# An attention-and-FFN kernel whose hash test moves into the contraction of its scores, in another layout, with its reciprocals through DRAM and in a free order

## The chip, the cores and the metric

The kernel runs on one core of a Trainium2 chip. The metric is the device time of one execution in microseconds (us), lower is better. The kernel before and the changed kernel were timed alternately; "before" and "changed" below always mean these two. Times are medians of all runs, slow ones too; a ratio is the mean time of one kernel's fast runs over that of the other's fast runs of the same rounds on the same chip, so it is not quite the ratio of the medians that stand beside it. Engines: PE is TensorE, DVE is VectorE, ACT is ScalarE, POOL is GpSimd, SP is the engine that only issues DMAs.

## The reference

Attention over 4 batches, 8 heads, 768 positions and 64 dimensions, in which a query sees only the keys of the same hash bucket (six sign bits), followed by a maxout FFN.

```python
q_bits = (np.einsum('bhsd,dk->bhsk', q, proj) > 0)      # proj: 64 x 6
k_bits = (np.einsum('bhsd,dk->bhsk', k, proj) > 0)
mask   = q_bucket[:, :, :, None] == k_bucket[:, :, None, :]
scores = np.where(mask, scale * q @ k.T, -1e9)
attn   = exp(scores - max) / sum                          # then attn @ v
h      = np.maximum(np.maximum(x @ w1, x @ w2), x @ w3)   # x: 3072 x 512, w: 512 x 768
out    = h @ w_out
```

## The kernel before

Its work comes in 16 phases (batch, four heads, half of the queries). In each phase PE makes the scores of the present phase in six groups, and between the groups it does the denominators and AV of the phase before and pieces of the FFN of the batch before. The order on every engine is the order of the source (`manual_schedule`). The 64 dimensions of a head lie as two blocks of 32 rows, so that four heads fill the 128 rows and a third round adds the hash test: a mismatch in any of 12 rows (six bits and their complements) adds -512.

```python
    def qk_group(ph, b, pp, half, c):
        scs = [scp.tile([P, 2, 512], FP32, tag="sc", name="sc") for _ in (0, 1)]
        qs = slice(half * HS, half * HS + HS)
        ks = slice(c * P, c * P + P)
        kT = tr["k", b, pp][:].bitcast(BF16).rearrange("p a (n two) -> p a n two", two=2)[:, :, :, 1]
        qT = tr["q", b, pp][:].bitcast(BF16).rearrange("p a (n two) -> p a n two", two=2)[:, :, :, 1]
        for rnd in range(3):
            for g in range(4):
                rows = slice(32 * g, 32 * g + 32)
                if rnd < 2:
                    l, r = kT[rows, rnd, ks], qT[rows, rnd, qs]
                else:
                    l, r = bits["k", b, pp][rows, ks], bits["q", b, pp][rows, qs]
                nc.tensor.matmul(scs[g // 2][:, g % 2, 0:HS], l, r, start=(rnd == 0), stop=(rnd == 2))
        for jj in (0, 1):
            nc.scalar.activation(atile(ph, jj, c)[:, :, 0:HS], scs[jj][:, :, 0:HS], ActFn.Exp, scale=SCALE)
```

The denominators are summed by PE with a matrix of ones, so each of four row groups of 32 holds one head. Their reciprocal and its broadcast over 64 rows stay on chip: 32x32 transposes on VectorE, and eight small copies on GpSimd.

```python
    def den(ph, b, pp, half):
        ps = bank()
        for c in range(NCH):
            for jj in (0, 1):
                for hd in (0, 1):
                    g = 2 * jj + hd
                    nc.tensor.matmul(ps[32 * g : 32 * g + 32, 0:HS], ones32[:],
                                     atile(ph, jj, c)[:, hd, 0:HS],
                                     start=(c == 0), stop=(c == NCH - 1))
        ds = dp.tile([P, HS], FP32, tag="ds", name="ds")
        nc.vector.tensor_scalar(out=ds[:], in0=ps[:, 0:HS], scalar1=float(S) * EPS, scalar2=None, op0=AluOp.add)
        dT = dp.tile([P, HS // 32, 32], FP32, tag="dT", name="dT")
        nc.vector.transpose(dT[:].rearrange("p a x -> p (a x)"), ds[:])
        rc = dp.tile([P, HS // 32], FP32, tag="rc", name="rc")
        nc.vector.reciprocal(rc[:], dT[:, :, 0])
        for jj in (0, 1):
            r2 = dp.tile([P, HS // 32], FP32, tag=f"r2{jj}", name=f"r2{jj}")
            for hd in (0, 1):
                for e in (0, 1):
                    o = 64 * hd + 32 * e
                    s = 32 * (2 * jj + hd)
                    nc.gpsimd.tensor_copy(r2[o : o + 32, :], rc[s : s + 32, :])
            rb = dp.tile([P, HS], FP32, tag=f"rb{jj}", name=f"rb{jj}")
            nc.vector.transpose(rb[:].rearrange("p (a x) -> p a x", x=32),
                                r2[:, :, None].to_broadcast([P, HS // 32, 32]))
            rcb[ph, jj] = rb
```

AV then multiplies by this `rb` while it leaves PSUM (`xT = (AV + eps * sum(v)) * rb`):

```python
# ... (matmuls into ps left out)
        nc.vector.scalar_tensor_tensor(
            out=xT[b][:, 2 * pp + jj, half * HS : half * HS + HS], in0=ps[:, 0:HS],
            scalar=sv[:, 0:1], in1=rcb.pop((ph, jj))[:], op0=AluOp.add, op1=AluOp.mult)
```

The hidden tile of the FFN gets its first value by a cast (`h`, line 281, on VectorE except in the tail) and two maxima on VectorE (line 284). The whole kernel:

The softmax here doesn't subtract the row's maximum and nothing guards it: scores larger than these inputs give would overflow.

## Time and profile before

366.1 us median (365.8 to 371.4, four runs; the longest is a slow run, over 1.5% above the fastest); one profiled run spans 363.1 us. The first fence is from the page of the kernel before: the span, busy time by engine, and four rows of the 40 time slices (tenths busy; the last is the granted clock of PE in tenths).

```profile
span 363.1 us, 7556 instructions
...
PE 300.6 (83%) x3166; PEld 131.1 (36%) x3166; DVE 203.4 (56%) x364; ACT 162.3 (45%) x223; POOL 39.1 (11%) x176
...
PE   5688688669797886989898795979998897999685
...
DVE  1625987665536668557245877567345554273531
ACT  1169289135556352510666653520496654701121
...
PEclk9689999899989996999989999899999998999999
```

PE is busy 83% of the span and is the engine to look at. But a busy PE is not a full one: matmuls overlap, so the groups below have 334 ns as the mean of one matmul though they start 162 ns apart. The costliest groups (line, engine, operation, output<-inputs, shapes, count | busy us, mean ns | idle before):

```profile
L272 PE MATMUL wk<-xT,w_sb 128*128 128x384 f16 x540 | 107.2, 334 | 30.2 <-DVE h_1882 L281 3.8
...
L202 PE MATMUL sc<-qT,kT 32*128 32x384 bf16 x768 | 59.8, 344 | 10.9 <-DVE bx L178 2.3
...
L202 PE MATMUL sc<-qb,kb 32*128 32x384 bf16 x384 | 37.4, 332 | 0.1
...
L167 PE MATMUL bps<-qT,pmq 32*32 32x384 f32 x256 | 21.6, 552 | 5.8 <-DVE sv L259 4.3
...
L150 DVE STREAM_TRANSPOSE kT<-knat 128x768 f32<-128x768 f32 (+1 forms) x18 | 25.1, 1437 | 0.0
```

The timeline around 200 us shows what a score group costs (start, duration, engine, line, operation, count):

```profile
start us, us, engine line op out<-in xcount [idle before <-releaser]
...
199.70 0.34 PE L202 MATMUL sc<-qT,kT 32*128 32x384 bf16 x4
199.87 0.33 PE L202 MATMUL sc<-qb,kb 32*128 32x384 bf16 x4
...
200.13 0.82 PE L272 MATMUL wk<-xT,w_sb 128*128 128x384 f16 x4
...
200.88 0.73 PE L202 MATMUL sc<-qT,kT 32*128 32x384 bf16 x8
```

Four heads' matmuls start at once, in four groups of 32 rows, and the next four 0.17 us later. The step to the FFN (line 272), which uses the whole array, takes 0.26 us (199.87 to 200.13) instead of some 0.16.

Since busy time misleads, I also split the time between PE's first and last matmul in three, from the trace: **wait** is the time in which no matmul was in flight (gaps over 50 ns); **clock** is half of the rest that lies in stretches of halved clock; **own** is what is left: the matmuls at their pace, with the changes of array mode. For the kernel before: own 285.6, clock 14.8, wait 57.3 us.

### The profile page before, as it was taken

How to read it: one execution, taken by the hardware profiler on the slowest of the kernel's cores; microseconds unless marked ns; L12 is line 12 of the kernel's file. 1: busy time of each engine (PE TensorE's matmuls, PEld its weight loads, DVE VectorE, ACT ScalarE, POOL GpSimd, SP SyncE). 2: the span in 40 equal slices, each digit the busy share in tenths (PEclk: the TensorE clock that was granted, in tenths of full speed). 3: DMA queues.
4: the chain of work that ended last, by engine and by line, in shares of the span. 5: the costliest groups of instructions: out<-in, count | busy, mean ns of one | idle time of the engine just before them, and what ended most of it. 6: DMA issues, size and time to landing. Idle time of an engine off the chain costs nothing. (4 is left out here: it accounts for less than half of the span.)

```text
span 363.1 us, 7556 instructions
## 1 busy us (share of the span) xinstructions
PE 300.6 (83%) x3166; PEld 131.1 (36%) x3166; DVE 203.4 (56%) x364; ACT 162.3 (45%) x223; POOL 39.1 (11%) x176
## 2 busy tenths in 40 slices
PE   5688688669797886989898795979998897999685
PEld 1123133224343432445343342335443342454342
DVE  1625987665536668557245877567345554273531
ACT  1169289135556352510666653520496654701121
POOL 7003013010301011000103103000011101000100
PEclk9689999899989996999989999899999998999999
DMA  8999243132025103130563003111200000102002
GB/s 181 296 302 199 36 185 44 29 123 93 10 52 198 49 2 43 40 106 10 183 253 45 2 0 45 60 51 46 88 2 0 2 3 0 70 19 88 2 0 87
DMA packets 17858, 27.62 MB, mean 76 GB/s; under 512 B 1952, under 2 KB 12960, under 8 KB 17824
## 3 DMA queue, kind: packets, MB, share of 16 engines
q1 hardware_dynamic: 10784, 20.85, 16.1%
q0 software_dynamic: 6720, 6.29, 11.0%
q8 instruction: 24, 0.39, 0.5%
q14 instruction: 10, 0.08, 0.1%
q10 hardware_dynamic: 320, 0.01, 0.0%
HBM read 25.17 MB, written 6.29 MB: 87 GB/s over the span
## 5 line engine op out<-in xcount | busy, mean ns | idle before, releaser
L272 PE MATMUL wk<-xT,w_sb 128*128 128x384 f16 x540 | 107.2, 334 | 30.2 <-DVE h_1882 L281 3.8
L272 PEld LDWEIGHTS <-w_sb 128*128 128x128 f16 x576 | 53.1, 98 | 89.8 <-issue 58.4
L202 PE MATMUL sc<-qT,kT 32*128 32x384 bf16 x768 | 59.8, 344 | 10.9 <-DVE bx L178 2.3
L292 ACT COPY o<-wk 128x512 f32<-128x512 f32 x23 | 13.5, 586 | 64.4 <-PE wk L289 44.1
L202 PE MATMUL sc<-qb,kb 32*128 32x384 bf16 x384 | 37.4, 332 | 0.1
L202 PEld LDWEIGHTS <-kT 32*128 32x128 bf16 x768 | 15.1, 94 | 53.2 <-issue 48.6
L255 PEld LDWEIGHTS <-v 128*64 128x64 f16 x384 | 20.3, 112 | 17.8 <-issue 11.4
L167 PE MATMUL bps<-qT,pmq 32*32 32x384 f32 x256 | 21.6, 552 | 5.8 <-DVE sv L259 4.3
L167 PE MATMUL bps<-kT,pmk 32*32 32x384 f32 x256 | 20.8, 553 | 5.9 <-DVE kT L150 4.0
L150 DVE STREAM_TRANSPOSE kT<-knat 128x768 f32<-128x768 f32 (+1 forms) x18 | 25.1, 1437 | 0.0
L150 DVE STREAM_TRANSPOSE qT<-qnat 128x768 f32<-128x768 f32 (+1 forms) x18 | 24.7, 1387 | 0.0
L259 DVE TENSOR_SCALAR sv<-wk 128x1 f32<-128x1 f32 x31 | 4.9, 157 | 33.6 <-PE wk L255 33.6
L231 DVE TENSOR_SCALAR ds<-wk 128x384 f32<-128x384 f32 x15 | 8.3, 556 | 25.6 <-PE wk L227 25.6
L202 PEld LDWEIGHTS <-kb 32*128 32x128 bf16 x384 | 12.9, 94 | 7.5 <-issue 1.5
L204 ACT ACTIVATE at_127<-sc 128x768 f16<-128x768 f32 x8 | 6.5, 815 | 18.7 <-PE sc L202 18.6
L204 ACT ACTIVATE at_159<-sc 128x768 f16<-128x768 f32 x8 | 6.5, 814 | 18.7 <-PE sc L202 18.7
L204 ACT ACTIVATE at_171<-sc 128x768 f16<-128x768 f32 x8 | 6.5, 814 | 16.0 <-PE sc L202 15.9
L178 DVE TENSOR_SCALAR kb<-bps,thrk 128x384 bf16<-128x384 f32 x10 | 6.2, 617 | 12.8 <-PE bps L167 12.8
L227 PEld LDWEIGHTS <-ones_121 128*32 128x32 f16 x384 | 8.9, 96 | 9.0 <-issue 5.5
L167 PEld LDWEIGHTS bps<-kT,pmk 32*32 32x32 f32 x256 | 6.7, 110 | 14.3 <-DVE kT L150 5.0
L85 POOL DMA_DIRECT2D v<-in_v_dram x16 | 11.6, 726 | 0.8 <-POOLq L400 0.8
L204 ACT ACTIVATE at_143<-sc 128x768 f16<-128x768 f32 x8 | 6.5, 814 | 11.4 <-PE sc L202 11.4
(440 smaller groups left out, 529.0 us busy)
## 6 DMA issues: line engine op xcount, KB each, us to landing
out_dram<-o SPq DMA_DIRECT2D x24, 256.0 KB, 2.0
knat<-in_k_dram SPq DMA_DIRECT2D x7, 768.0 KB, 5.2
qnat<-in_q_dram SPq DMA_DIRECT2D x7, 768.0 KB, 7.5
v<-in_v_dram POOLq DMA_DIRECT2D x16, 192.0 KB, 4.0
w_sb<-in_moe_w_dram POOLq DMA_DIRECT2D x3, 768.0 KB, 23.2
qb<-bx SPq DMA_DIRECT2D x14, 72.0 KB, 2.0
knat<-in_k_dram SPq DMA_DIRECT2D x2, 384.0 KB, 6.5
qnat<-in_q_dram SPq DMA_DIRECT2D x2, 384.0 KB, 9.0
```

The source lines that it names most:

```text
L85: nc.gpsimd.dma_start(t[:].rearrange("p h c d -> p h (c d)"), v[b, 2 * j : 2 * j + 2].rearrange("h (p c) d -> p h (c d)", p=P))
L150: nc.vector.transpose(t[:, blk, c0 * P : c1 * P].rearrange("p (c i jj) -> p jj c i", jj=4, i=32), n[:].rearrange("p (jj c x) -> p jj c x", ...
L167: nc.tensor.matmul(ps[o : o + 32, :], pm[nm][32 * g : 32 * g + 32, blk, :], tr[nm, b, pp][32 * g : 32 * g + 32, blk, cs], start=(blk == 0) ...
L178: nc.vector.tensor_scalar(out=d, in0=ps, scalar1=thr[nm][:, 0:1], scalar2=(1.0 if nm == "q" else MISS), op0=AluOp.is_gt, op1=AluOp.mult)
L202: nc.tensor.matmul(scs[g // 2][:, g % 2, 0:HS], l, r, start=(rnd == 0), stop=(rnd == 2))
L204: nc.scalar.activation(atile(ph, jj, c)[:, :, 0:HS], scs[jj][:, :, 0:HS], ActFn.Exp, scale=SCALE)
L227: nc.tensor.matmul(ps[32 * g : 32 * g + 32, 0:HS], ones32[:], atile(ph, jj, c)[:, hd, 0:HS], start=(c == 0), stop=(c == NCH - 1))
L231: nc.vector.tensor_scalar(out=ds[:], in0=ps[:, 0:HS], scalar1=float(S) * EPS, scalar2=None, op0=AluOp.add)
L255: nc.tensor.matmul(ps[D * hd : D * hd + D, 0 : HS + 1], vv[:, hd, c, :], atile(ph, jj, c)[:, hd, :], start=(c == 0), stop=(c == NCH - 1))
L259: nc.vector.tensor_scalar(out=sv[:], in0=ps[:, HS : HS + 1], scalar1=EPS, scalar2=None, op0=AluOp.mult)
L272: nc.tensor.matmul(ps[:, 0:HS], w_sb[m][:, jc, fb * P : fb * P + P], xT[b][:, jc, half * HS : half * HS + HS], start=(jc == 0), stop=(jc = ...
L292: nc.scalar.copy(o[:], ps[:, 0:DM])
```

## The change

Each head gets a full pass of the array: its 64 dimensions and its 12 hash rows lie side by side in one operand of 76 rows (first head of a pair) or 128 rows (second head: hash rows, zeros, dimensions). With it come other changes: batch 0 is transposed by PE instead of VectorE, phases are pairs of heads (both query halves), PSUM is one pool of four two-bank tiles, the first cast of `h` is always on ScalarE, q and k are loaded by GpSimd with overlapping rows, the reciprocal goes through three DMA steps and DRAM (the last step is four broadcasts), and `manual_schedule` is gone, so that the framework orders the instructions of each engine by its own estimate ("free order"). The core of the diff:

```diff
-    scp = ctx.enter_context(tc.tile_pool(name="scp", bufs=3, space=bass.MemoryType.PSUM))
-    wkp = ctx.enter_context(tc.tile_pool(name="wkp", bufs=2, space=bass.MemoryType.PSUM))
-    ctx.enter_context(tc.manual_schedule())
+    drp = ctx.enter_context(tc.tile_pool(name="drp", bufs=3, space=bass.MemoryType.DRAM))
+    psp = ctx.enter_context(tc.tile_pool(name="psp", bufs=4, space=bass.MemoryType.PSUM))
 ...
+    HROW = (D, 0)
+    KROWS = (slice(0, D + 2 * NBITS), slice(0, P))
 ...
+    def hash_bits(b, js):
+        pst = [psum2("bps") for _ in js]
+        for half in (0, 1):
+            cs = slice(half * HS, half * HS + HS)
+            for x, (j, ps) in enumerate(zip(js, pst)):
+                for hd in (0, 1):
+                    rows = slice(D * hd, D * hd + D)
+                    for z, nm in enumerate(("q", "k")):
+                        o = 32 * (2 * (hd ^ x) + z)
+                        nc.tensor.matmul(ps[o : o + 32, half, 0:HS], pm[nm][rows, :],
+                                         oset(b, j)[nm, hd][rows, cs], start=True, stop=True)
+        # ... one VectorE op makes the bits (bt), four DMAs put them into the operands' hash rows
 ...
+    def qk_unit(ph, b, j, half, c):
+        sc = psum2("sc")
+        for hd in (0, 1):
+            rows = KROWS[hd]
+            kT = oset(b, j)["k", hd].bitcast(BF16)[:, 1::2]
+            qT = oset(b, j)["q", hd].bitcast(BF16)[:, 1::2]
+            nc.tensor.matmul(sc[:, hd, 0:HS], kT[rows, c * P : c * P + P],
+                             qT[rows, half * HS : half * HS + HS], start=True, stop=True)
+        nc.scalar.activation(atile(ph, half, c)[:, :, 0:HS], sc[:, :, 0:HS], ActFn.Exp, scale=SCALE)
 ...
     def den(ph):   # after the matmuls with ones
+        nc.scalar.copy(ds[:], ps[:, 0:HS])
+        E = HS // 32
+        cd = dp.tile([P, E], FP32, tag="cd", name="cd")
+        nc.sync.dma_start(cd[:], ds[0:P:32, :].rearrange("g (m e) -> g m e", e=E))
+        rc = dp.tile([P, E], FP32, tag="rc", name="rc")
+        nc.vector.tensor_scalar(out=rc[:], in0=cd[:], scalar1=float(S) * EPS, scalar2=None, op0=AluOp.add)
+        nc.vector.reciprocal(rc[:], rc[:])
+        rd = drp.tile([4, HS], FP32, tag="rd", name="rd")
+        nc.sync.dma_start(rd[:].rearrange("g (m e) -> (g m) e", e=E), rc[:])
+        for half in (0, 1):
+            rb = dp.tile([P, HS], FP32, tag=f"rb{half}", name=f"rb{half}")
+            for hd in (0, 1):
+                g = 2 * half + hd
+                nc.sync.dma_start(rb[D * hd : D * hd + D, :], rd[g : g + 1, :].to_broadcast([D, HS]))
+            rcb[ph, half] = rb
 ... (loads, transposes, output DMAs and the order of emission are left out)
```

## The prediction

> **What bounds the kernel now.** The engine table gives PE 300.6 us of a 363.1 us span, DVE 203, ACT 162. But PE is not working all that time. From the timeline, undisturbed start-to-start paces are 162 ns for a full-array 384-column matmul, 165 ns for a group of four row- or column-tiled ones, and 216 ns for a 512-column one. The change of array mode adds about 95 ns (252 to 260 ns instead of 162); the Trainium skill, "TensorEngine Tiling (Array Packing)", section "Key Properties", says that changing the tiling mode drains the engine, and the trace agrees. At those paces all PE work is about 245 us. The rest is waiting: 57 us of PE gaps over 0.1 us, about 18 us for 200 mode changes, some 10 us of halved clock (mean 0.952), a 17 us start before the first exponential, and PE waiting on DVE evictions behind 1.6 us transposes (1 to 4 us gaps before the first FFN layer).
> By exponentials in the timeline: start 17 us, batch 0 57 us, twelve later phases 20.1 us each, tail 47 us.
>
> **What the change does on PE.** Scores: 288 groups of four (47.5 us at pace) become 384 full-array passes, 62 us: 15 us MORE ideal work, although the record of busy time (97 us) suggests a saving. Hash: 512 records become 256, in 64-row tiles of four at a time: about 25 us instead of 32. Transposes of batch 0: 48, estimated 5 to 10 us. FFN, denominators and AV keep 93+31+15+31 us. Total about 265 us. Scores now share the mode of the FFN; mode changes in the built order fall only from 201 to 170.
>
> **Elsewhere.** DVE: transposes 48 x 1.57 = 75 us (was 50, two heads per instruction now), but denominator transposes, broadcast transposes and the h casts leave: about 190 us in all. ACT: 192 x 0.81 + 48 x 0.48 casts + 24 x 0.59 + 16 x 0.48 = about 200 us. The reciprocal path now crosses three DMAs (each about 2 us to landing in the DMA issues), about 11 us from the denominators to xT; the order leaves room for most of it. q/k are read twice for batches 1 to 3.
>
> **Critical path, estimated.** Start 21 us (256-byte loads, transposes, hash and the DMA of hash rows before the first score). Phases 0 to 4 have no FFN and are bound by ACT: 12 x 0.81 + 0.5 = 10.2, so about 11 us each, plus 3 to 5 us because the loads of pairs 1 and 2 come late and PE is in order: ends near 80 us (before: 93). Eleven phases with FFN: qk 4.0 + den 1.0 + AV 2.0 + hash 1.5 + FFN 7.7 + mode changes 0.8 = 17 us of PE; with 8% for waits and clock, 18.4: 202 us. Tail: 40 us FFN plus latency, 46 us.
> Sum 328 us. So the gain comes from the free order, the shared PSUM pool (four two-bank tiles instead of three plus two single banks) and a fuller batch 0, not from the score pass.
>
> **Prediction 328 us, 80% range 308 to 349. Faster by over 2%: 0.88; within 2%: 0.08; slower: 0.04.**
>
> **What would show it.** Score matmuls at 162 ns pace; PE total at pace higher, gaps halved; exponentials back to back in the first five phases; no 1 to 4 us gaps before the first FFN layer; phases of 18 to 19 us; tail unchanged.
>
> **What would make it wrong.** xT waiting for the broadcast DMA and blocking the in-order DVE queue, so that maxima, PSUM tiles and PE wait (phases of 20 us or more); late 256-byte loads stalling the start past 30 us; strided score operands slower at full array; or, to the good, hardly any waits (310 us).

## The result, and the profile after

The changed kernel takes 435.6 us median (429.7 to 438.0, four runs, of which that of 438.0 counts as slow) against 366.1: ratio 1.185, 95% interval 1.170 to 1.200. It is 18% slower; 328 us had been predicted. From its page, the rows that answer to those of before:

```profile
span 434.2 us, 5976 instructions
...
PE 354.0 (82%) x2186; PEld 158.9 (37%) x2186; DVE 160.8 (37%) x290; ACT 188.7 (43%) x281; POOL 105.7 (24%) x223
...
PE   6489496929399789679797997979698799799994
...
DVE  5073331331235462344325334434414432233341
ACT  1064356605236365245364272626255167432231
...
PEclk9596857976679999699889698969789699999999
```

VectorE and ScalarE are far from full (37% and 43%), PE is as busy as before by its share, and the clock row has 5s, 6s and 7s in 13 of its 40 slices where the kernel before had two 6s and otherwise 8s and 9s: the mean granted clock is 0.865, where it was 0.952. The groups:

```profile
L294 PE MATMUL wk<-xT,w_sb 128*128 128x384 f16 x576 | 120.4, 344 | 12.1 <-DVE xT L284 7.9
...
L220 DVE TENSOR_SCALAR bt<-bps,thr,fac 128x768 f32<-128x768 f32 x16 | 17.2, 1077 | 60.3 <-PE bps L216 60.3
...
L239 PE MATMUL sc<-qop_0_126,kop_0_123 76*128 76x384 bf16 x72 | 26.3, 366 | 9.4 <-DMA kop_0_123<-bt 6.5
...
L239 PE MATMUL sc<-qop_0_127,kop_0_124 128*128 128x384 bf16 x72 | 26.3, 368 | 0.0
...
L216 PE MATMUL bps<-qop_0_126,pmq 64*32 64x384 f32 x24 | 12.6, 619 | 9.1 <-DVE qop_0_126 L202 6.9
```

The split of PE's time: own 309.2 (before 285.6), clock 44.7 (14.8), wait 74.3 (57.3). So of 71 us, 24 are more work on PE, 30 are a slower clock and 17 more waiting. By line, the 24 are the hash matmuls (22 to 35 us), the scores (68 to 74), the new transposes on PE (6) and small changes elsewhere, with the FFN's first layer 5 us cheaper.

What does PE wait for? One phase, from the timeline of all engines ("SPq" is the issue of a DMA; in brackets the idle time before an instruction and what ended it):

```profile
start us, us, engine line op out<-in xcount [idle before <-releaser]
...
297.16 0.33 PE L251 MATMUL wk<-at_187,ones_117 128*32 128x384 f16 x2
...
297.59 0.48 ACT L255 COPY ds<-wk 128x384 f32<-128x384 f32 x1 [2.44 <-PE wk L251]
...
300.08 0.59 SPq L258 DMA_DIRECT2D cd<-ds  x1
...
302.87 0.55 DVE L303 TENSOR_TENSOR h_2638<-h_2638,wk 128x384 f16<-128x384 f16 x1 [1.38 <-PE wk L294]
...
303.34 0.17 DVE L260 TENSOR_SCALAR rc<-cd 128x12 f32<-128x12 f32 x1
...
303.53 0.34 PE L278 MATMUL wk<-at_185,v 128*64 128x385 f16 x2
...
303.79 0.32 SPq L263 DMA_DIRECT2D rd<-rc  x1
...
305.29 1.15 SPq L268 DMA_DIRECT2D rb_2591<-rd  x2
...
309.38 0.62 DVE L284 SCALAR_TENSOR_TENSOR xT<-wk,sv,rb_2591 128x384 f16<-128x384 f32 x1 [3.42 <-DMA rb_2591<-rd]
309.91 0.96 DVE L202 STREAM_TRANSPOSE qop_2_138<-qnat 64x768 f32<-64x768 f32 x1
310.05 1.37 PE L294 MATMUL wk<-xT,w_sb 128*128 128x384 f16 x4 [3.49 <-DVE xT L284]
...
311.35 0.85 PE L216 MATMUL bps<-qop_2_138,pmq 64*32 64x384 f32 x1
...
311.45 0.56 DVE L303 TENSOR_TENSOR h_2638<-h_2638,wk 128x384 f16<-128x384 f16 x1 [0.58 <-PE wk L294]
```

The denominators' last matmuls start at 297.16. Then: copy by ScalarE; DMA issue at 300.08 behind others in SP's queue; VectorE's `rc` at 303.34; the DMA to DRAM at 303.79; the broadcasts at 305.29; and `xT` at 309.38. That is some 12 us, as estimated. But `xT` stands in VectorE's in-order queue, and VectorE idles 3.42 us in front of it, while the transpose `qop_2_138` (309.91) stands behind it; the hash matmul (311.35) follows that transpose. PE's gap of 3.49 us ends with `xT` itself. Its matmuls (310.05) make the last of a hidden tile's three products; the other two were made before (the first maximum on `h_2638` is at 302.87, the second at 311.45), so they do not need this `xT`. By the source, what they share with it is the PSUM pool: AV's result was complete at 303.9 (its last matmuls are at 303.53), and its PSUM tile (a buffer of the accumulator memory) stayed occupied until `xT` read it, 5.5 us later. The same in the view of waits (who waited for what: us in total, times, longest):

```profile
engine line waited for: us in total, times, longest us
...
DVE rc L260 <- DMA cd<-ds: 23.2, 6, 8.0
...
PE wk L251 <- DVE xT L284: 8.5, 1, 8.5
PE wk L294 <- DVE xT L284: 7.9, 5, 3.5
...
PE wk L278 <- DVE xT L284: 7.4, 2, 6.3
...
DVE xT L284 <- DMA rb_907<-rd: 5.4, 1, 5.4
DVE xT L284 <- DMA rb_755<-rd: 5.4, 1, 5.4
```

The broadcasts are listed one by one; over all of them VectorE idled 37.2 us before `xT`, which with the 23.2 us before `rc` makes 60 us. PE's gaps that `xT` ended sum to 26 us. The 8.5 us (line 251, denominators) and 7.4 us (line 278, AV) stand before matmuls that never read `xT`: by the source, they too can wait only for a PSUM tile. And the clock follows the gaps: the trace grants half clock from 310.2 us for 6.8 us, right after this gap of 3.49 us, and all eleven gaps over 2 us lie in such a stretch or end less than 1 us before one. The Trainium skill, "TensorE: Matmul & The Clock Gate", section "HAM oscillation — how this bites in real kernels", gives this as the rule "no PE-idle gaps >~3.4µs"; this trace agrees in kind, with shorter gaps: one of 2.31 us that ended at 285.9 us was followed by 6.8 us of half clock. The length of a gap does not settle it: in the kernel before, two gaps of 2.44 us (ended at 80.3 and 118.5 us) had no half clock within 7 us. That the gaps cause the halving is an inference from their places; no run here forced the clock.

### The profile page after: what moved, and what is told of

It reads as the page before. It is cut to its first block, busy times and chain, and to the rows that moved or that the text cites. A ratio compares the mean times of both kernels' runs of the same rounds, so it can differ in the third digit from the quotient of the medians.

```text
span 434.2 us, 5976 instructions
## 1 busy us (share of the span) xinstructions
PE 354.0 (82%) x2186; PEld 158.9 (37%) x2186; DVE 160.8 (37%) x290; ACT 188.7 (43%) x281; POOL 105.7 (24%) x223
## 4 chain that ended last, share of the span: by engine, by line
PE 62%; DMA 21%; DVE 8%; issue 4%; SPq 3%; ACT 3%; DVEq 0%; ACTq 0%
PE wk L294 20%; PE sc L239 13%; PE bps L216 10%; DMA cd<-ds 7%; PE wk L310 7%; PE wk L278 5%; PE wk L251 5%; DMA rd<-rc 5%; SPq L268 2%; DMA rb_758<-rd 1%; DVE xT L284 1%; DMA rb_1939<-rd 1%; PE wps L345 1%; DMA kop_0_123<-bt 1%; PE trp L190 1%
## 5 line engine op out<-in xcount | busy, mean ns | idle before, releaser
L294 PE MATMUL wk<-xT,w_sb 128*128 128x384 f16 x576 | 120.4, 344 | 12.1 <-DVE xT L284 7.9
L96 POOL DMA_DIRECT2D v<-in_v_dram x48 | 25.3, 538 | 152.7 <-PE wk L278 150.4
L220 DVE TENSOR_SCALAR bt<-bps,thr,fac 128x768 f32<-128x768 f32 x16 | 17.2, 1077 | 60.3 <-PE bps L216 60.3
L327 POOL DMA_DIRECT2D out_dram<-o x20 | 10.8, 549 | 99.5 <-ACT o L315 99.5
L239 PE MATMUL sc<-qop_0_126,kop_0_123 76*128 76x384 bf16 x72 | 26.3, 366 | 9.4 <-DMA kop_0_123<-bt 6.5
L81 POOL DMA_DIRECT2D qnat<-in_q_dram x48 | 23.3, 498 | 40.3 <-DVE qop_2_139 L202 13.7
L239 PE MATMUL sc<-qop_1_132,kop_1_129 76*128 76x384 bf16 x60 | 23.0, 383 | 7.0 <-DVE bt L220 4.9
L239 PE MATMUL sc<-qop_0_127,kop_0_124 128*128 128x384 bf16 x72 | 26.3, 368 | 0.0
L81 POOL DMA_DIRECT2D knat<-in_k_dram x48 | 23.8, 514 | 1.8 <-DMA qnat<-in_q_dram 1.2
L239 PE MATMUL sc<-qop_2_138,kop_2_135 76*128 76x384 bf16 x60 | 22.3, 371 | 0.9 <-ACT at_183 L241 0.6
L239 PE MATMUL sc<-qop_1_133,kop_1_130 128*128 128x384 bf16 x60 | 22.9, 381 | 0.0
L239 PE MATMUL sc<-qop_2_139,kop_2_136 128*128 128x384 bf16 x60 | 21.9, 366 | 0.0
L241 ACT ACTIVATE at_187<-sc 128x768 f16<-128x768 f32 x8 | 6.5, 815 | 34.8 <-PE sc L239 34.8
L216 PE MATMUL bps<-qop_0_126,pmq 64*32 64x384 f32 x24 | 12.6, 619 | 9.1 <-DVE qop_0_126 L202 6.9
L216 PE MATMUL bps<-qop_1_132,pmq 64*32 64x384 f32 x20 | 10.6, 615 | 10.2 <-DVE qop_1_132 L202 6.8
L241 ACT ACTIVATE at_163<-sc 128x768 f16<-128x768 f32 x8 | 6.5, 817 | 24.9 <-PE sc L239 24.9
```

The lines of the kernel that those rows point to most:

```text
L81: eng.dma_start(t[32 * g : 32 * g + 32, 0 : R * D - 32], s[:, 32 * blk : 32 * blk + R * D - 32])
L96: nc.gpsimd.dma_start(tv[32 * jj : 32 * jj + 32], s4[jj])
L216: nc.tensor.matmul(ps[o : o + 32, half, 0:HS], pm[nm][rows, :], oset(b, j)[nm, hd][rows, cs], start=True, stop=True)
L220: nc.vector.tensor_scalar(out=bt[:].rearrange("p (a n) -> p a n", a=2), in0=ps[:, :, 0:HS], scalar1=thr[:, 0:1], scalar2=fac[:, 0:1], op0= ...
L239: nc.tensor.matmul(sc[:, hd, 0:HS], kT[rows, c * P : c * P + P], qT[rows, half * HS : half * HS + HS], start=True, stop=True)
L241: nc.scalar.activation(atile(ph, half, c)[:, :, 0:HS], sc[:, :, 0:HS], ActFn.Exp, scale=SCALE)
```

## The experiments

Theory A: the reciprocal's round trip through DMAs makes VectorE, then PE, wait, and the gaps halve the clock. Rival B: the free order is bad in itself. Rival C: the new score and hash passes need more PE time. The runs came in three (1 to 4, 5 to 8, 9 to 12), each on another chip; the kernel before had medians of 369.0, 368.0 and 367.0 us there, so compare ratios. All results were correct. The medians and the split of PE's time in each profiled run:

| run | median us | ratio to before | own | clock | wait |
|---|---|---|---|---|---|
| before | 366.1 | 1 | 285.6 | 14.8 | 57.3 |
| changed | 435.6 | 1.185 | 309.2 | 44.7 | 74.3 |
| 1 changed, reciprocal on chip | 382.3 | 1.041 | 312.0 | 19.2 | 44.4 |
| 2 before, reciprocal by DMAs | 383.7 | 1.046 | 287.9 | 17.8 | 70.3 |
| 3 changed, manual order | 492.7 | 1.340 | 298.4 | 42.2 | 146.1 |
| 4 changed, on chip and manual | 445.5 | 1.215 | 299.0 | 26.2 | 108.7 |
| 5 before, free order | 359.9 | 0.977 | 292.9 | 17.0 | 42.9 |
| 6 run 1, hash emitted later | 413.6 | 1.126 | 309.8 | 31.8 | 63.9 |
| 7 run 1, 128 rows for both heads | 384.8 | 1.047 | 310.1 | 17.5 | 49.5 |
| 8 changed, AV emitted later | 444.6 | 1.208 | 306.1 | 45.1 | 87.5 |
| 9 changed, DMA waits off VectorE | 389.2 | 1.075 | 305.3 | 19.1 | 54.4 |
| 10 run 1, hash of head 2 first | 369.6 | 1.021 | 297.8 | 11.7 | 52.7 |
| 11 before, free order, casts on ScalarE | 353.2 | 0.975 | 292.1 | 16.3 | 37.9 |
| 12 before, casts on ScalarE | 356.3 | 0.983 | 286.5 | 17.6 | 50.3 |

### 1. The changed kernel with the reciprocal on chip

```diff
-        nc.scalar.copy(ds[:], ps[:, 0:HS])
-        # cd by DMA, add, reciprocal, rd by DMA to DRAM, rb by four DMAs
+        nc.vector.tensor_scalar(out=ds[:], in0=ps[:, 0:HS], scalar1=float(S) * EPS, scalar2=None, op0=AluOp.add)
+        nc.vector.transpose(dT[:].rearrange("p a x -> p (a x)"), ds[:])
+        nc.vector.reciprocal(rc[:], dT[:, :, 0])
+        # per half: four nc.vector.tensor_copy into r2, one nc.vector.transpose into rb
```

> The changed kernel with one part undone: the reciprocal of the denominators goes back on chip (VectorE transposes and eight small VectorE copies instead of three DMAs through DRAM); free order kept. Theory A (the DMA round trip holds xT, VectorE and then PE, and each such gap halves the clock): 370 to 395 us, PE gaps over 50 ns fall from 74 to under 40 us and the time at half clock from 116 to under 60 us. Rival B (the free order itself is bad) and rival C (the score and hash passes simply need more PE time): 415 us or more.

382.3 us: 53 of the 70 us are gone, as A said; B and C alone are out as the main cause. PE's waits fell from 74 to 44 us (just short of the "under 40" expected) and its half-clock time from 117 to 43.5 us, although VectorE does more (214 us busy instead of 161). The clock term of the split fell by 25.5 and the wait by 30 us: together they are the gain, nearly half of it by the clock. PE's gaps that `xT` ended fell from 26 to 2 us, most of the 30; the waits for the transposes of the hash stayed:

```profile
PE bps L216 <- DVE qop L202: 12.5, 9, 3.6
...
PE wk L251 <- DVE xT L285: 0.9, 1, 0.9
...
PE wk L279 <- DVE xT L285: 0.5, 1, 0.5
```

### 2. The kernel before with the reciprocal by DMAs

The reverse edit, in manual order.

> The kernel before with one part done alone: its reciprocal goes through the three DMAs of the changed kernel; manual order and everything else kept. Theory A: slower by 20 us or more (385 to 430 us), with waits of xT for the broadcast DMA. Rivals B and C: within 2% of before (360 to 373 us).

383.7 us, ratio 1.046 (1.033 to 1.059): slower, but by some 15 to 17 us, under the 20 expected. The same two waits appear on VectorE:

```profile
DVE rc L237 <- DMA cd<-ds: 79.0, 16, 11.6
...
DVE xT L262 <- DMA rb<-rd: 29.1, 16, 4.7
```

There they sum to 108 us, more than in the changed kernel, and cost PE only 13 us of wait and 3 of clock. So a wait on VectorE is not yet a loss: it depends on what PE needs of it. Here PE's gaps that `xT` ended rose from 3 to 18 us, far less than the 108.

### 3 and 4. The changed kernel in manual order, with DMAs and with the reciprocal on chip

```diff
+    ctx.enter_context(tc.manual_schedule())
```

> The changed kernel in the order in which its source emits it (manual order), the DMA round trip kept. Rival B: 370 to 395 us. Theory A: 420 us or more, since the emitted order leaves about five score units (some 8 us) between denominators and AV. Rival C: 420 us or more.

> Both undone: reciprocal on chip and emitted order. If only A holds, the same as the run with the reciprocal on chip alone, within 2%. If A and B both hold, 15 us or more below it. If C holds, still 400 us or more.

492.7 and 445.5 us. Rival B is wrong in sign: the free order saves 57 us with the DMAs and 63 without. In the emitted order PE waits 84 and 69 us before the matmuls of the FFN's first layer, as the split by line shows. That run 4 lies far above run 1 had not been expected; the emission of this source was evidently never meant to be the order. But own time is lower in manual order (299 against 312 us), 9 us of it because the hash matmuls take 26 us instead of 35; run 10 takes that up.

### 5. The kernel before in free order

```diff
-    ctx.enter_context(tc.manual_schedule())
```

> The kernel before with the manual order taken away, nothing else. The emitted order cost the changed kernel 57 us (493 against 436 us) and 63 us with the reciprocal on chip; if a free order is a gain by itself, and not only a repair of this change's emission, this run is faster than before by 3% or more (350 us or less), its 57 us of PE gaps falling below 40 us. If the emission of the kernel before was already well placed: within 2% of before.

359.9 us, ratio 0.977 (0.970 to 0.984): 2.3% faster, a smaller gain than the 3% named. Waits fell from 57 to 43 us (not below 40), and own time rose by 7, with the score groups up from 68 to 77 us.

### 6. On top of run 1: hash passes emitted later

```diff
-                add(u + 2, hash_bits, nb, [nj])
+                add(u + 5, hash_bits, nb, [nj])
...
-                add(u + 9, hash_bits, nb, [nj])
+        if 4 <= ph + 1 < len(pairs):
+            nb, nj = pairs[ph + 1]
+            add(3, hash_bits, nb, [nj])
```

> On top of the run with the reciprocal on chip (382 us): the hash passes are emitted later, a phase after their transposes (batches 1 to 3) and three units later (batch 0). Theory A2 (of what is left, some 21 us is PE in order waiting at hash matmuls for transposes): wait before hash matmuls falls from 21 us to under 10, time 365 to 374 us. Rival (the rest is extra PE work: hash tiles in three slots, 172 ns score passes, transposes): within 1% of 382 us.

413.6 us: a clear miss, 31 us slower. The wait before hash matmuls doubled from 21 to 41 us. The timeline of one phase tells why:

```profile
start us, us, engine line op out<-in xcount [idle before <-releaser]
...
194.44 0.56 DVE L255 TENSOR_SCALAR ds<-wk 128x384 f32<-128x384 f32 x1 [4.45 <-PE wk L251]
...
196.84 0.97 DVE L204 STREAM_TRANSPOSE kop<-knat 64x768 f32<-64x768 f32 x1
...
200.33 1.93 DVE L202 STREAM_TRANSPOSE qop<-qnat 64x768 f32<-64x768 f32 x2
...
201.40 0.74 PE L216 MATMUL bps<-qop,pmq 64*32 64x384 f32 x1 [5.03 <-DVE qop L202]
```

VectorE idles 4.45 us for the denominators' matmuls (`ds`), with the transposes of the next pair behind them in its queue; PE comes to the hash matmul of that pair and waits 5.03 us for the last of the transposes. Emitting the hash later had let the free order place its transposes later too. The spare time went into another order, not into slack.

### 7. On top of run 1: 128 rows for both heads

```diff
-                if hd == 1:
-                    nc.gpsimd.memset(t[0:D, :], 0.0)
+                z = slice(0, D) if hd == 1 else slice(D, P)
+                nc.gpsimd.memset(t[z, :], 0.0)
...
-    KROWS = (slice(0, D + 2 * NBITS), slice(0, P))
+    KROWS = (slice(0, P), slice(0, P))
```

> On top of the run with the reciprocal on chip: the score pass of the first head uses all 128 rows (the unused ones set to zero once) instead of 76, so that all score passes have one shape. If the 76-row pass beside a 128-row one is what makes the score pace 172 to 175 ns instead of 162, the pace falls to 162 to 165 and the time by 2 to 5 us; if not, no change (within 0.5%).

384.8 us, no gain; the pace of most score matmuls at full clock went from 171 to 176 ns to 169 to 172 ns, not to 162. The 76 rows are worth some 3 ns of it at most. In the kernel before, the two score rounds that read every other bf16 element also start their next four after 170 ns or, more often, some 183, and the full-array FFN matmuls, whose operands are dense, 162; the stride fits, but was not tested alone.

### 8. The changed kernel with AV emitted later

```diff
-            u0 = 8 if b == 0 else 6
+            u0 = 9
```

> The changed kernel, DMA round trip kept, but AV emitted three score units later (one in batch 0), so that part of the round trip is hidden rather than taken away. Theory A: 405 to 428 us, PE gaps 74 us fall to 50 to 68. If the round trip's latency is not the cause: within 1% of 436 us.

444.6 us, a miss: hiding the latency behind a later AV made things slightly worse. VectorE's idle time on the two DMAs rose from 60 to 79 us: its waiting instructions stay where the free order puts them. The theory in the form "the latency is too long for the room it has" falls; what remains is "the wait on VectorE holds up others", which run 9 tests. (The edit did reach the built order: the score units between denominators and AV rose from between four and six to seven or eight in most phases.)

### 9. The changed kernel with its DMAs, and no wait for them on VectorE

```diff
-        nc.vector.tensor_scalar(out=rc[:], in0=cd[:], scalar1=float(S) * EPS, scalar2=None, op0=AluOp.add)
-        nc.vector.reciprocal(rc[:], rc[:])
+        nc.gpsimd.tensor_scalar(out=rc[:], in0=cd[:], scalar1=float(S) * EPS, scalar2=None, op0=AluOp.add)
+        nc.gpsimd.tensor_tensor(out=rc[:], in0=rc[:], in1=one12[:], op=AluOp.pow)   # one12 holds -1
...
-        nc.vector.scalar_tensor_tensor(out=xT[...], in0=ps[:, 0:HS], scalar=sv[:, 0:1],
-                                       in1=rcb.pop((ph, half))[:], op0=AluOp.add, op1=AluOp.mult)
+        nc.vector.tensor_scalar(out=raw[:], in0=ps[:, 0:HS], scalar1=sv[:, 0:1], scalar2=None, op0=AluOp.add)
+        nc.gpsimd.tensor_tensor(out=xT[...], in0=raw[:], in1=rcb.pop((ph, half))[:], op=AluOp.mult)
```

> The changed kernel with its three DMAs kept, but nothing that waits for them left on VectorE: VectorE evicts AV at once into SBUF, and GpSimd does the reciprocal and the multiplication into xT. Theory A-queue (what costs is that instructions waiting for a DMA stand in VectorE's in-order queue ahead of transposes and evictions that PE waits for): 375 to 405 us, VectorE idle time on these DMAs 60 us falls to 0, half-clock time well below 116 us. Rival A-latency (xT itself comes too late for what PE does next): still 420 us or more. It can fail for another reason: GpSimd's queue also issues the loads, which may now come late.

389.2 us: with the three DMAs kept, 46 of the 70 us are gone by the medians, some 40 by the ratios. No VectorE instruction waits for `cd` or `rb` any more. So it is VectorE's waiting for the DMAs, much more than the latency of `xT`, that cost the time. But the edit does two things at once: it takes the waits out of VectorE's queue, and it frees AV's PSUM tile at once, since VectorE evicts AV without the reciprocal. Which of the two counts more, no run separates; the traces, where the gaps ended by `xT` make up 24 of the 30 us of wait that run 1 gave back, speak for the PSUM tile. Latency still shows, where PE needs `xT` at once; PE's longest waits are now

```profile
PE wk L297 <- POOL xT L288: 21.7, 3, 9.8
```

three of them, the longest 9.8 us, where the FFN of a finished batch starts. That and the load issues sharing GpSimd's queue may make up the 7 us to run 1 (12 by the ratios); this was not taken apart. The Trainium skill says in "TensorE: Matmul & The Clock Gate", section "Architectural detail: the array is 16× 32×32, not 1× 128×128", that the queues of ScalarE and VectorE are strict FIFO (first in, first out). The changed kernel's trace fits that: VectorE idled 3.42 us in front of `xT` and began the transpose behind it only then (309.91).

### 10. On top of run 1: the second head's hash matmuls first

```diff
-                for hd in (0, 1):
+                for hd in (1, 0):
```

> On top of the run with the reciprocal on chip (382 us): the hash matmuls of the second head are emitted first, so that the free order no longer splits the eight of a pair into two and six; they then run in two sets of four tiles instead of three. Expected if PE's own work counts: own PE time of hash matmuls 35 us falls to 26, wait before them 21 us to 10 to 20, time 366 to 377 us. If PE's own work is not what is left: within 1% of 382 us.

369.6 us, 2.1% above the kernel before (1.021, 1.010 to 1.031). With the first head first, the free order issued two of a pair's eight hash matmuls as soon as that head was transposed and the rest later, so the eight ran in three sets instead of two. Now own time of the hash matmuls fell from 35.3 to 23.4 us. The wait before them stayed at 24 us (10 to 20 expected), but the clock term fell to 11.7. From run 1 to this run own time fell by 14 us and the clock term by 7.5, while wait rose by 8. So rival C is part of the truth: after run 1 the split had own time 26 us above the kernel before and wait 13 us below it, and this run takes away about half of what was left by the ratios (4.1% to 2.1%, with intervals that just overlap).

### 11 and 12. The kernel before with two of the smaller steps

```diff
-            if tail["on"]:
-                nc.scalar.copy(h[:], ps[:, 0:HS])
-            else:
-                nc.vector.tensor_copy(h[:], ps[:, 0:HS])
+            nc.scalar.copy(h[:], ps[:, 0:HS])
```

Run 11 has free order as well.

> The kernel before with free order and with the first cast of each hidden tile on ScalarE, as the changed kernel has it (two of its smaller steps, none of its layout, score pass or DMA round trip). Free order alone gave 360 us. Expected 345 to 357 us if VectorE evictions are what PE waits for in the FFN; within 1% of 360 us if not.

> The kernel before, manual order kept, only the first cast of each hidden tile moved to ScalarE. Its PE gaps before the first FFN layer are 33 us, most of them ended by this cast on VectorE. Expected 345 to 360 us and that wait below 20 us; if ScalarE's exponentials in front of the cast make it as late as VectorE's transposes did: within 1% of before.

353.2 us (ratio 0.975, 0.963 to 0.987) and 356.3 us (0.983, 0.971 to 0.996). Both beat both kernels. The wait before the first layer fell from 33 to 22 us in run 12 (its profile fell in a slow run, so this number is rough, and it is above the 20 expected). By ratio, run 11 is not distinct from run 5 (0.975 against 0.977): the medians 353 and 360 come from different chips. What is shown is that steps this change brought along make the old layout about 2% faster (1.7 to 2.5% in runs 5, 11 and 12).

## Why the prediction was wrong

- **"about 11 us from the denominators to xT; the order leaves room for most of it": the step that failed.** The latency was right (some 12 us in the phase shown); that the order hides it was not. Two VectorE instructions wait for DMAs, 60 us in all. Meanwhile AV's result holds its PSUM tile and transposes stand behind in the queue, and PE waits: 26 us until `xT` was done (2 us in run 1). Taking the DMAs away (run 1) gave back 53 us, taking only their waits off VectorE and evicting AV at once (run 9) 40 to 46 us. More room before AV (run 8) did not help. How much of it is the held tile and how much the queue was not separated. The prediction named this as what could make it wrong, and gave it almost no weight (0.04 for slower).
- **"with 8% for waits and clock": mis-sized.** Waits and clock were 119 us, over a quarter of the span. Gaps of 2 to 9 us per phase came with 3 to 14 us of half clock each; half-clock time was 117 us instead of 35. The clock term alone is 30 us of the 71.
- **"Total about 265 us" of PE work: mis-sized by 44 us;** own time was 309. About 16 us of this are mode changes (170 at 95 ns), which the prediction counted apart and only in part (0.8 us a phase). Hash was put at 25 us and took 35 (22 in the kernel before), because the free order split the sets; run 10 reached 23. Scores were put at 62 and took 74, at a pace of mostly 171 to 176 ns instead of 162.
- **"15 us MORE ideal work" in the scores: right in kind.** At full clock four heads mostly took 183 + 170 + 161 = 514 ns in row groups and take 4 x 174 = 696 ns in full passes, 17 us more over 96 units. With the mode changes around them, the trace has the scores at 68 and 74 us. The score pass, the change's main idea, was never a gain on PE: four heads of 32 rows already shared the array. FFN matmuls got about 5 us cheaper (105.7 to 100.6), which fits with fewer mode changes beside the scores.
- **"Phases 0 to 4 ... bound by ACT ... ends near 80 us": wrong.** They ended at 123.5 us. ScalarE was busy under half of the time from 20 to 120 us. Run 1 still needed 102 us, with half clock for 31 of its first 58 us; why the clock stays down there was not tested.
- **"transposes 48 x 1.57 = 75 us": mis-sized.** A transpose of 64 rows took 0.97 us, 47 us in all. VectorE was less loaded than thought, and still made PE wait: what VectorE waits for, not its load.
- **"the gain comes from the free order": right as a direction.** Free order saved 57 us here (run 3) and 2.3% before (run 5). It could not outweigh the rest.

## What to carry to other kernels

An instruction that waits for a DMA costs by what it holds back: the PSUM tile that it has still to read, and what stands behind it in its engine's queue. Keep round trips off the engine that empties PSUM for PE, or on chip. Before merging passes that use part of the array, check whether they already run side by side; the pace of starts tells it, and busy time does not. And price a gap on PE at more than its length, since here the granted clock fell around most gaps of over 2 us (not all, and the cause is inferred).

## What the Trainium skill lacked or had wrong

- "TensorE: Matmul & The Clock Gate", section "HAM oscillation — how this bites in real kernels", has a rule for idle gaps over some 3.4 us; here a gap of 2.31 us (changed kernel, ended at 285.9 us) was followed by 6.8 us of half clock, while two of 2.44 us in the kernel before were not. Which gap brings the halving stays open.
- The same page, section "Back-to-back issue gap", gives N / 2.4 + 2.5 ns as the isolated gap of a warm matmul of N columns, 162.5 ns at 384. Here dense matmuls agree (161 to 163 ns), but score matmuls that read every other bf16 element mostly started 169 to 176 ns apart. No page gives a pace for these; the stride as its cause was not tested alone.
- "TensorEngine Tiling (Array Packing)", section "Key Properties", says that a change of tiling mode drains the engine, without a size; here it added about 95 ns (some 257 instead of 162 ns to the next start).
- "DMA: Bandwidth & Descriptors", section "Anatomy of one DMA — SWDGE (gpsimd) path", gives a fixed cost of about 2.0 us per DMA for DMAs that GpSimd issues, so about 6 us for three in a row (an estimate from that section). No page gives the time of such a chain as a kernel sees it: here, issued by SP, with a copy, VectorE's part and SP's queue between them (`cd` alone was issued 2.0 us after the copy ended, behind DMAs of hash rows), it took some 12 us from the denominators to `xT`.
